# Attention, then a mixture of experts: five key chunks of each first tile of a pair and four of each second one are transposed by DMA, one and two by TensorE

## The chip, the cores and the metric

The kernel runs on one core of a Trainium2 chip. A time is the device time of one execution in microseconds (us); less is better. Of the runs of a kernel the median counts. A profiled execution, which has a time of its own, gave the trace.

## The reference

`q` holds 4 x 12288 queries of width 128. `kv` (4 x 384 x 32 x 128) is averaged over 4 x 4 blocks, which leaves 768 keys a batch, and multiplied by `w_sr`; the result serves as keys and as values. Then a top-1 mixture of experts with 8 experts follows on the 49152 rows.

```python
kv_flat = kv.reshape(B, H // 4, 4, W // 4, 4, C).mean(axis=(2, 4)).reshape(B, -1, C) @ w_sr
s = (q @ kv_flat.transpose(0, 2, 1)) / np.sqrt(C)
a = np.exp(s - s.max(-1, keepdims=True))
a /= a.sum(-1, keepdims=True) + 1e-09
x = (a @ kv_flat).reshape(B * S, D)
do_compute = x @ w_skip > 0
e = argmax(x @ w_gate); gate = softmax(x @ w_gate)[e]
out = x + do_compute * gate * (relu(x @ w1[e]) @ w2[e])
```

## The kernel before

The attention stage goes over 384 tiles of 128 queries, 96 a batch. Everything is kept to nearly float32 precision by splitting operands into a high and a low part, so one product becomes three matmuls. In step t of the loop the program records, in this order on each engine: the scores of tile t (`scores`, TensorE, six matmuls L636 to L638 into `s_ps`, two PSUM buffers); the value product of tile t-6 (`attend`, 18 matmuls, L701); the TensorE transposes of tile t-1 (`p_transpose`, L676); the row maximum of tile t on VectorE (`row_max`, L644, `nm`); the high part of tile t-1 on ScalarE (`p_hi`, L654); the exponential of tile t on ScalarE (`row_exp`, L650, `p_sb`); the low part of tile t-1 on VectorE (`p_lo`, L658), and behind it, on SyncE's queue, a DMA that transposes (L663). The order is the program's own; a schedule is not searched.

The value product needs the 128 x 768 probabilities of a tile transposed, in six chunks of 128 keys. They go two ways. Of the first `KD` = 4 chunks `p_hi` and `p_lo` make a float16 high and low part in a staging tile (`p16`, written `p` in the trace, four buffers), and one DMA transposes both, eight blocks of 128 x 128, into `pt` (six buffers), which `attend` reads six steps later. The other two chunks TensorE transposes in float32 into a PSUM tile that the two tiles of a pair (`PP` = 2) share; one step after the pair is complete ScalarE (L683) and VectorE (L684) split all four of them into high and low float16 parts in `ptq`. So a step with an odd t handles the first tile of a pair in `p_hi` and `p_lo`, and also the `ptq` parts of the pair before.

Between these stand, by rules of the loop, the splits of the queries (L619, L622, each fourth tile), the pooling of the next batch's keys on GpSimd, the routing of finished rows (each twelfth tile) and the scatter of rows to their expert's list (L191, GpSimd). SyncE's queue carries the loads of queries (L605) and keys (L460), the stores of the attention's rows (L719) and the transposing DMAs, in program order.

The second part, from about 960 us on, is the MoE stage: 128-row tiles of each expert's list, `up` (L294 to L298), `down` (L309), `finish` (L321), and its own transposing DMA (`xT<-x`, eight blocks too).

Of the kernel before, what the change touches and what calls it, by code (L numbers as in the profile page):

```python
# [12 lines left out]
F16 = mybir.dt.float16  # L13
# [12 lines left out]
def kernel(  # L26
# [11 lines left out]
    nc = tc.nc  # L38
    NR, C, RT, P = q.shape
    B = kv.shape[0]  # L40
    NQ = NR * RT * P // B
    KC, R = kv.shape[1], kv.shape[2]
# [23 lines left out]
    LAG = 6  # L66
    WARM = 6
    PSL = 11
    KD = 4
    PP = 2  # L70
    L1, L2, PW, PX = 11, 8, 1, 1
    ROW = C + 4
# [14 lines left out]
    ident = consts.tile([P, P], F32, name="ident")  # L87
# [296 lines left out]
    def acc_ps():  # L384
        return ps_a.tile([P, 512], F32, name="acc_ps")
# [34 lines left out]
    with ExitStack() as p1:  # L420
# [7 lines left out]
        ptp = p1.enter_context(tc.tile_pool(name="ptp", bufs=LAG))  # L428
        ptq = p1.enter_context(tc.tile_pool(name="ptq", bufs=4))
        hl = p1.enter_context(tc.tile_pool(name="hl", bufs=4))  # L430
# [167 lines left out]
        q_sb, qT, PT, AVT, ROWS, P_SB, S_PS, P16, PTP, PTQ = ({} for _ in range(10))  # L598
# [51 lines left out]
            nc.scalar.activation(out=P_SB[t], in_=S_PS.pop(t)[:, :, :HK], func=AF.Exp, bias=NM.pop(t))  # L650

        def p_hi(t):
            P16[t] = hl.tile([P, 2, KD * P], F16, name="p16")
            nc.scalar.activation(out=P16[t][:, 0, :], in_=p_flat(t)[:, 0:KD * P], func=AF.Copy, scale=2.0 ** PEXP)  # L654

        def p_lo(t):
            p16 = P16.pop(t)
            paced["both"] = nc.vector.scalar_tensor_tensor(  # L658
                out=p16[:, 1, :], in0=p_flat(t)[:, 0:KD * P], scalar=2.0 ** PEXP, in1=p16[:, 0, :], op0=ALU.mult,
                op1=ALU.subtract).ins  # L660
            P_SB.pop(t)
            PT[t] = ptp.tile([P, 2 * KD, P], F16, name="pt")
            nc.sync.dma_start_transpose(PT[t], p16.rearrange("p a x -> p (a x)"))  # L663

        def p_flat(t):
            return P_SB[t].rearrange("p h x -> p (h x)")

        KP = KC - KD

        def p_transpose(t):  # L670
            g, j = divmod(t, PP)
            if j == 0:
                PTP[g] = acc_ps()
            p = p_flat(t)
            for i in range(KP):
                nc.tensor.transpose(PTP[g][:, (j * KP + i) * P:(j * KP + i + 1) * P],  # L676
                                    p[:, (KD + i) * P:(KD + i + 1) * P], ident)
            if j < PP - 1:
                return
            ps = PTP[g][:, 0:PP * KP * P]  # L680
            hl_t = ptq.tile([P, 2, PP * KP * P], F16, name="ptq")
            PTQ[g] = hl_t.rearrange("p a (j k x) -> p a j k x", j=PP, x=P)
            next_a.append(lambda: nc.scalar.activation(out=hl_t[:, 0, :], in_=ps, func=AF.Copy, scale=2.0 ** PEXP))  # L683
            next_v.append(lambda: nc.vector.scalar_tensor_tensor(  # L684
                out=hl_t[:, 1, :], in0=ps, scalar=2.0 ** PEXP, in1=hl_t[:, 0, :], op0=ALU.mult, op1=ALU.subtract))
# [3 lines left out]
        def attend(t):  # L689
            g, j = divmod(t, GT)  # L690
            r, o = divmod(g, RG)
            v_hi, v_lo, v_sc = *KV[t // TPB][2:4], KV[t // TPB][4][:, 0:1]
            v = (v_hi, v_lo)
            if j % 2 == 0:
                AVT[g] = acc_ps()[:, 0:2 * XW].rearrange("p (a x) -> p a x", x=XW)
            ps = AVT[g]
            pt = PT.pop(t)
            ptq_t = PTQ[t // PP]
            for i, (k, a, x) in enumerate(AVL):
                w = pt[:, x * KD + k, :] if k < KD else ptq_t[:, x, t % PP, k - KD, :]  # L700
                nc.tensor.matmul(ps[:, j % 2, :], w, v[a][:, k, :], start=(i == 0), stop=(i == len(AVL) - 1))  # L701
            if j == 0:
                if o == 0:
                    ROWS[r] = rowp.tile([P, RT, XW], F32, name="rows")
            rows = ROWS[r][:, o * GT:(o + 1) * GT, :]
            rs = small.tile([P, 2], F32, name="rs") if j % 2 == 1 else None

            def inverse():
                nc.vector.tensor_scalar(out=rs, in0=ps[:, :, XW - 1], scalar1=1e-9 * 2.0 ** PEXP, scalar2=v_sc,  # L709
                                        op0=ALU.add, op1=ALU.mult)  # L710
                nc.vector.reciprocal(rs, rs)

            def scale():
                for i in (0, 1):
                    c = j - 1 + i
                    nc.scalar.activation(out=rows[:, c, :], in_=ps[:, i, :], func=AF.Copy, scale=rs[:, i:i + 1])
                if j < GT - 1:
                    return
                nc.sync.dma_start(ov[r][:, o * GT:(o + 1) * GT, :], rows[:, :, 0:C])  # L719
                if o == RG - 1:  # L720
                    jobs.append([route(r), None])

            if j % 2 == 1:
                early_v.append(inverse)
                next_l.append(scale)
# [223 lines left out]
        t = -1  # L949
        while t < NTILE + LAG:  # L950
# [8 lines left out]
            for u in (t - LAG,) if live else (2 * t - NTILE - LAG, 2 * t - NTILE - LAG + 1):  # L959
                if 0 <= u < NTILE:  # L960
                    attend(u)
            if 0 <= t - 1 < NTILE:
                p_transpose(t - 1)
# [4 lines left out]
            if 0 <= t - 1 < NTILE:  # L968
                p_hi(t - 1)
# [5 lines left out]
            if 0 <= t - 1 < NTILE:  # L975
                p_lo(t - 1)
# [135 lines left out]
```

## Time and profile before

| | us |
|---|---|
| runs: median (lowest to highest of 3) | 1744.91 (1743.05 to 1745.06) |
| the profiled execution's own time | 1749.1 |
| its span in the trace | 1747.4 |
| TensorE busy, all of the span | 1703.9 |
| VectorE busy, all of the span | 1533.4 |
| ScalarE busy, all of the span | 1264.5 |
| attention stage, first scores to last | 21 to 958 |

A busy time is the union of an engine's instructions. TensorE's are pipelined with modelled ends, so its busy time says that something was in flight, not that the engine was at its peak.

### The profile page before, as it was taken

The page shows a single profiled execution, that of the slowest core. Times are in us where ns is not written, and L with a number is a line of the kernel's source. Part 1 is how long each engine was busy: PE and PEld are TensorE (multiplying, and loading weights), DVE is VectorE, ACT ScalarE, POOL GpSimd, SP SyncE. Part 2 cuts the span into 40 slices and gives each one's busy share as a digit, 9 for nine tenths or more (in the row PEclk, how much of TensorE's full clock was granted, in tenths as well). Part 3 has the DMA queues.
Part 4 walks back from the last instruction along what each step waited for, and adds up shares of the span by engine and source line. Part 5 has one row for each costly group of instructions (what it writes and reads, how often), then busy time and mean ns, then how long its engine had stood idle before and what let it go on. Part 6 is the DMA issues. An engine that isn't in the chain of part 4 may idle for free.

```text
span 1747.4 us, 51304 instructions
## 1 busy us (share of the span) xinstructions
PE 1703.9 (98%) x18789; PEld 1425.9 (82%) x18789; DVE 1533.4 (88%) x3240; ACT 1264.5 (72%) x2399; POOL 989.9 (57%) x1256
## 2 busy tenths in 40 slices
PE   5999999999999999999999999999999999999998
PEld 3999999999999999999998777777777777777776
DVE  7999999999999999999998777767888888888887
ACT  3888888888888888888888555555566555666664
POOL 2268767888677778565657544444433333334433
PEclk9999999999999999999999999999999999999999
DMA  6999999999799999899998675223433343333333
GB/s 214 236 227 209 201 202 223 226 202 186 171 197 205 224 221 196 186 200 197 204 204 177 161 206 132 85 83 82 94 98 97 100 104 98 97 100 108 99 97 86
DMA packets 616916, 281.18 MB, mean 161 GB/s; under 512 B 502944, under 2 KB 567072, under 8 KB 616736
## 3 DMA queue, kind: packets, MB, share of 16 engines
q1 hardware_dynamic: 590192, 231.68, 64.3%
q0 software_dynamic: 21504, 38.43, 6.8%
q10 hardware_dynamic: 5040, 8.72, 1.3%
q8 instruction: 106, 1.74, 0.4%
q14 instruction: 74, 0.61, 0.1%
HBM read 85.36 MB, written 79.72 MB: 94 GB/s over the span
## 4 chain that ended last, share of the span: by engine, by line
PE 81%; DVE 14%; issue 3%; POOL 1%; DMA 1%; ACT 1%; DVEq 0%; POOLq 0%; SPq 0%; ACTq 0%
PE acc_ps L309 22%; PE acc_ps L701 17%; PE s_ps L636 6%; PE s_ps L638 5%; PE s_ps L637 5%; PE h_ps L294 5%; PE h_ps L295 5%; PE h_ps L296 5%; DVE nm L644 5%; PE acc_ps L676 3%; DVE p L658 3%; PE up_ps L294 2%; PE up_ps L295 2%; PE up_ps L296 2%; DVE ptq L684 2%
## 5 line engine op out<-in xcount | busy, mean ns | idle before, releaser
L191 POOL DMA_INDIRECT scr<-rows,di x384 | 422.8, 1101 | 205.9 <-DVE nm L644 133.0
L650 ACT ACTIVATE p_sb<-s_ps,nm 128x768 f32<-128x768 f32 x384 | 346.4, 902 | 116.5 <-DVE nm L644 103.8
L644 DVE TENSOR_REDUCE nm<-s_ps 128x1 f32<-128x768 f32 x384 | 365.5, 952 | 23.2 <-PE s_ps L638 10.5
L191 POOL DMA_INDIRECT out_dram<-o,xin x196 | 201.4, 1028 | 315.5 <-DVE o L321 266.9
L297 ACT ACTIVATE h_hi<-h_ps 128x512 f16<-128x512 f32 x384 | 223.9, 597 | 208.0 <-PE h_ps L296 194.3
L701 PEld LDWEIGHTS <-pt 128*128 128x128 f16 x4608 | 274.9, 97 | 63.2 <-issue 62.7
L701 PE MATMUL acc_ps<-v_hi,pt 128*128 128x138 f16 x3072 | 320.4, 224 | 1.4 <-DVE rs L709 0.9
L309 PEld LDWEIGHTS <-h_hi 128*128 128x128 f16 x4608 | 288.0, 98 | 17.6 <-issue 1.7
L636 PE MATMUL s_ps<-k_hi,q_hi 128*128 128x384 f32 x768 | 294.4, 383 | 0.4 <-ACT k_hi L511 0.4
L701 PE MATMUL acc_ps<-v_lo,pt 128*128 128x138 f16 x1536 | 293.1, 223 | 0.0
L658 DVE SCALAR_TENSOR_TENSOR p<-p_sb,p 128x512 f16<-128x512 f32 x384 | 271.3, 706 | 2.4 <-ACT p L654 1.1
L298 DVE SCALAR_TENSOR_TENSOR h_lo<-h_ps,h_hi 128x512 f16<-128x512 f32 x384 | 245.7, 687 | 19.8 <-ACT h_hi L297 17.7
L638 PE MATMUL s_ps<-k_hi,q_lo 128*128 128x384 f32 x768 | 260.2, 339 | 0.0
L637 PE MATMUL s_ps<-k_lo,q_hi 128*128 128x384 f32 x768 | 258.7, 337 | 0.0
L654 ACT ACTIVATE p<-p_sb 128x512 f16<-128x512 f32 x384 | 242.1, 631 | 5.3 <-DMA pt<-p 1.8
L309 PE MATMUL acc_ps<-w_hi,h_lo 128*128 128x128 f16 x2304 | 223.1, 219 | 0.6 <-issue 0.5
L309 PE MATMUL acc_ps<-w_lo,h_hi 128*128 128x128 f16 x2304 | 211.8, 219 | 0.8 <-issue 0.7
L309 PE MATMUL acc_ps<-w_hi,h_hi 128*128 128x128 f16 x2304 | 210.9, 219 | 0.0
L297 ACT ACTIVATE h_hi<-up_ps 128x512 f16<-128x512 f32 x192 | 114.4, 597 | 113.5 <-PE up_ps L296 103.6
L701 PE MATMUL acc_ps<-v_hi,ptq 128*128 128x138 f16 x1536 | 178.1, 223 | 0.0
L321 DVE SCALAR_TENSOR_TENSOR o<-acc_ps,g_sc,xin 128x128 f32<-128x128 f32 x288 | 81.0, 344 | 107.1 <-PE acc_ps L309 107.1
L701 PE MATMUL acc_ps<-v_lo,ptq 128*128 128x138 f16 x768 | 155.0, 223 | 0.0
(190 smaller groups left out, 3367.0 us busy)
## 6 DMA issues: line engine op xcount, KB each, us to landing
q_sb<-in_q_dram SPq DMA_DIRECT2D x96, 256.0 KB
out_dram<-rows SPq DMA_DIRECT2D x96, 256.0 KB
xin<-scr SPq DMA_DIRECT2D x75, 264.0 KB, 2.9
kvt<-in_kv_dram SPq DMA_DIRECT2D x74, 256.0 KB
w_raw<-in_moe_w_dram SPq DMA_DIRECT2D x26, 512.0 KB, 4.0
scr<-pad ACTq DMA_DIRECT2D x32, 264.0 KB
pt<-p SPq DMA_TRANSPOSE x384
scr<-rows,di POOLq DMA_INDIRECT x384
```

The costliest lines, as they stand in the source:

```text
L191: ins = nc.gpsimd.indirect_dma_start(out=dst, out_offset=bass.IndirectOffsetOnAxis(ap=ids, axis=0), in_=src, in_offset=None, bounds_check= ...
L297: nc.scalar.activation(out=h["hi"][:, c, :], in_=ps, func=AF.Relu)
L298: paced["by"] = nc.vector.scalar_tensor_tensor(out=h["lo"][:, c, :], in0=ps, scalar=0.0, in1=h["hi"][:, c, :], op0=ALU.max, op1=ALU.subtra ...
L309: m = nc.tensor.matmul(ys[t], h[x][:, k, t * P:(t + 1) * P], w[:, k, :], start=(i == 0), stop=(i == len(terms) - 1))
L636: nc.tensor.matmul(s[:, h, :HK], q_hi, k_hi[:, sl], start=True, stop=False)
L637: nc.tensor.matmul(s[:, h, :HK], q_hi, k_lo[:, sl], start=False, stop=False)
L638: nc.tensor.matmul(s[:, h, :HK], q_lo, k_hi[:, sl], start=False, stop=True)
L644: paced["by"] = nc.vector.tensor_reduce(out=NM[t], in_=S_PS[t][:, :, :HK], axis=AX.XY, op=ALU.max, negate=True).ins
L650: nc.scalar.activation(out=P_SB[t], in_=S_PS.pop(t)[:, :, :HK], func=AF.Exp, bias=NM.pop(t))
L654: nc.scalar.activation(out=P16[t][:, 0, :], in_=p_flat(t)[:, 0:KD * P], func=AF.Copy, scale=2.0 ** PEXP)
L658: paced["both"] = nc.vector.scalar_tensor_tensor(out=p16[:, 1, :], in0=p_flat(t)[:, 0:KD * P], scalar=2.0 ** PEXP, in1=p16[:, 0, :], op0=A ...
L701: nc.tensor.matmul(ps[:, j % 2, :], w, v[a][:, k, :], start=(i == 0), stop=(i == len(AVL) - 1))
```

## The change

The number of chunks that the DMA transposes becomes a list over the place in the pair, `KDS = (5, 4)`, where it was 4 for both. A first tile then has one chunk left for TensorE, a second one two, so a pair's PSUM tile has three chunks where it had four. The tiles `p16` and `pt` are allocated at the larger size, 2 x 5 x 128 columns, and a second tile uses a part of them; `ptq` is allocated for three chunks.

```diff
-    KD = 4
+    KDS = (5, 4)
...
         def p_hi(t):
-            P16[t] = hl.tile([P, 2, KD * P], F16, name="p16")
+            KD = KDS[t % PP]
+            P16[t] = hl.tile([P, 2 * max(KDS) * P], F16, name="p16")[:, 0:2 * KD * P].rearrange("p (a x) -> p a x", a=2)
...
-            PT[t] = ptp.tile([P, 2 * KD, P], F16, name="pt")
+            PT[t] = ptp.tile([P, 2 * max(KDS), P], F16, name="pt")[:, 0:2 * KD, :]
...
-        KP = KC - KD
+        KP0 = [sum(KC - KDS[i] for i in range(j)) for j in range(PP + 1)]
...
-            for i in range(KP):
-                nc.tensor.transpose(PTP[g][:, (j * KP + i) * P:(j * KP + i + 1) * P],
-                                    p[:, (KD + i) * P:(KD + i + 1) * P], ident)
+            for i in range(KP0[j], KP0[j + 1]):
+                k = KDS[j] + i - KP0[j]
+                nc.tensor.transpose(PTP[g][:, i * P:(i + 1) * P], p[:, k * P:(k + 1) * P], ident)
...
-            ps = PTP[g][:, 0:PP * KP * P]
-            hl_t = ptq.tile([P, 2, PP * KP * P], F16, name="ptq")
+            ps = PTP[g][:, 0:KP0[PP] * P]
+            hl_t = ptq.tile([P, 2, KP0[PP] * P], F16, name="ptq")
...
-                w = pt[:, x * KD + k, :] if k < KD else ptq_t[:, x, t % PP, k - KD, :]
+                KD = KDS[t % PP]
+                w = pt[:, x * KD + k, :] if k < KD else ptq_t[:, x, KP0[t % PP] + k - KD, :]
```

The program's instructions before and after have the same places on VectorE and on SyncE's queue. On VectorE, in the middle of the attention stage, three steps before (`p` is the staging tile, `nm` the row maximum, `rs` the scale of finished rows):

```order
1006 L644 TENSOR_REDUCE nm<-s_ps 128x1
1007 L684 SCALAR_TENSOR_TENSOR ptq<-acc_ps,ptq 128x512
1008 L709 TENSOR_SCALAR rs<-acc_ps,v_x_sc 128x2
1009 L711 RECIPROCAL rs<-rs 128x2
1010 L658 SCALAR_TENSOR_TENSOR p_11172<-p_sb,p_11172 128x512
1011 L644 TENSOR_REDUCE nm<-s_ps 128x1
1012 L658 SCALAR_TENSOR_TENSOR p_11222<-p_sb,p_11222 128x512
```

and the same rows now:

```order
1006 L644 TENSOR_REDUCE nm<-s_ps 128x1
1007 L686 SCALAR_TENSOR_TENSOR ptq<-acc_ps,ptq 128x384
1008 L712 TENSOR_SCALAR rs<-acc_ps,v_x_sc 128x2
1009 L714 RECIPROCAL rs<-rs 128x2
1010 L660 SCALAR_TENSOR_TENSOR p_11061<-p_sb,p_11061 128x640
1011 L644 TENSOR_REDUCE nm<-s_ps 128x1
1012 L660 SCALAR_TENSOR_TENSOR p_11111<-p_sb,p_11111 128x512
```

The 128 columns left one instruction of a step and joined another of the same step; the next step is as it was.

On SyncE's queue, a stretch with loads of keys, queries and stores of rows between the transposing DMAs, before:

```order
202 L663 DMA_TRANSPOSE pt<-p_5571 128x8x128
203 L719 DMA out_dram<-rows 128x4x128
204 L663 DMA_TRANSPOSE pt<-p_5620 128x8x128
205 L460 DMA kvt<-in_kv_dram 128x512
206 L663 DMA_TRANSPOSE pt<-p_5670 128x8x128
207 L663 DMA_TRANSPOSE pt<-p_5715 128x8x128
```

and now:

```order
202 L665 DMA_TRANSPOSE pt<-p_5516 128x10x128
203 L722 DMA out_dram<-rows 128x4x128
204 L665 DMA_TRANSPOSE pt<-p_5565 128x8x128
205 L460 DMA kvt<-in_kv_dram 128x512
206 L665 DMA_TRANSPOSE pt<-p_5614 128x10x128
207 L665 DMA_TRANSPOSE pt<-p_5659 128x8x128
```

No DMA changes its place; each other one of the transposes has ten blocks where it had eight.

## Rows read from the trace of the kernel before

**Rows 1.** The page, busy us of each engine, its share of the span, instructions.
```profile
PE 1703.9 (98%) x18789; PEld 1425.9 (82%) x18789; DVE 1533.4 (88%) x3240; ACT 1264.5 (72%) x2399; POOL 989.9 (57%) x1256
```
**Rows 2.** Busy time of each engine in two stretches, granted clock, DMA share, GB/s.
```profile
core 0: us, PE busy (x) PEld busy (x) DVE busy (x) ACT busy (x) POOL busy (x), PEclk, DMA share, GB/s
40.50:917.80 877.30, 873.33 (x9523) 811.50 (x9521) 837.80 (x1640) 761.88 (x1401) 619.39 (x836) 1.00 1.02 205
917.80:958.00 40.20, 36.79 (x397) 33.67 (x394) 35.62 (x75) 32.85 (x64) 29.64 (x39) 1.00 0.90 177
```
**Rows 3.** The same view for the row maximum, L644, alone, with its count.
```profile
40.50:917.80 877.30, 344.18 (x362) 1.00 1.02 205
```
**Rows 4.** Chain that ended last, by line: 40.5:917.8, 285:314, 254.2:464.3, 917:960 us.
```profile
by line: PE acc_ps L701 32.3%; PE s_ps L636 10.7%; PE s_ps L638 10.6%; PE s_ps L637 10.4%; DVE nm L644 8.0%; PE acc_ps L676 6.5%; DVE p L658 5.2%; issue 4.0%; DVE ptq L684 2.9%; DVE q_lo L622 2.0%; DMA pt<-p 0.8%; POOL scr L191 0.7%; POOL e
by line: PE acc_ps L701 46.4%; PE s_ps L636 14.8%; PE s_ps L638 14.5%; PE s_ps L637 14.4%; PE acc_ps L676 9.8%; PE acc_ps L786 0.2%; PE acc_ps L785 0.2%
by line: DVE nm L644 19.4%; PE acc_ps L701 17.5%; DVE p L658 12.3%; issue 7.2%; DVE ptq L684 7.1%; PE s_ps L636 5.6%; PE s_ps L638 5.5%; PE s_ps L637 5.5%; DVE q_lo L622 4.8%; PE acc_ps L676 3.4%; POOL ev L747 2.6%; POOL scr L191 1.9%; DVE 
by line: DVE nm L644 23.3%; issue 13.5%; PE acc_ps L701 9.5%; DVE p L658 9.4%; DVE ptq L684 8.3%; DVE q_lo L622 5.3%; PE s_ps L638 4.7%; PE s_ps L636 4.2%; PE s_ps L637 4.0%; PE acc_ps L676 2.6%; POOL ev L747 2.6%; ACT p_sb L650 2.2%; DVE x
```
**Rows 5.** That chain in order of time, 500:510 us: start us, us, what.
```profile
502.98 1.09 PE acc_ps L701 x18
504.07 0.22 PE acc_ps L676 x2
504.30 0.18 PE s_ps L636
...
505.35 1.09 PE acc_ps L701 x18
```
**Rows 6.** Groups by line and shape: busy us, mean ns of one, idle before, releasers.
```profile
L644 DVE TENSOR_REDUCE nm<-s_ps 128x1 f32<-128x768 f32 x384 | 365.5, 952 | 23.2 <-PE s_ps L638 10.5 <-issue 7.8 <-PE acc_ps L701 3.2
L658 DVE SCALAR_TENSOR_TENSOR p<-p_sb,p 128x512 f16<-128x512 f32 x384 | 271.3, 706 | 2.4 <-ACT p L654 1.1 <-DMA pt<-p 1.0 <-issue 0.3
L654 ACT ACTIVATE p<-p_sb 128x512 f16<-128x512 f32 x384 | 242.1, 631 | 5.3 <-DMA pt<-p 1.8 <-issue 0.4 <-ACT q_hi L619 0.2
L676 PE MATMUL acc_ps<-ident,p_sb 128*128 128x128 f32 x768 | 148.3, 275 | 3.8 <-ACT p_sb L650 3.6
L684 DVE SCALAR_TENSOR_TENSOR ptq<-acc_ps,ptq 128x512 f16<-128x512 f32 x192 | 130.5, 680 | 0.3
L683 ACT ACTIVATE ptq<-acc_ps 128x512 f16<-128x512 f32 x192 | 112.8, 588 | 0.0
L283 DVE SCALAR_TENSOR_TENSOR x<-xin,x 128x128 f16<-128x128 f32 x296 | 84.2, 345 | 0.7 <-ACT x L280 0.7
L321 DVE SCALAR_TENSOR_TENSOR o<-acc_ps,g_sc,xin 128x128 f32<-128x128 f32 x288 | 81.0, 344 | 107.1 <-PE acc_ps L309 107.1
L274 DVE SCALAR_TENSOR_TENSOR w_lo<-w_raw,w_sc,w_hi 128x1024 f16<-128x1024 f32 x13 | 16.7, 1283 | 3.9 <-issue 3.6 <-ACT w_hi L273 0.3
```
**Rows 7.** ScalarE ahead of an exponential: waits 100:900 us in total; timeline of one.
```profile
ACT p_sb L650 <- DVE nm L644: 84.8, 211, 1.5
...
501.64 0.90 ACT L650 ACTIVATE p_sb<-s_ps,nm 128x768 f32<-128x768 f32 x1 [0.43 <-DVE nm L644]
```
**Rows 8.** Transposing DMAs: issue on SyncE ns, a key load, landing, waits 100:900.
```profile
L663 SPq DMA_TRANSPOSE pt<-p x88: 1231/1248/3040, 255.2 to 462.5; - x88
...
291.37 0.57 SPq L460 DMA_DIRECT2D kvt<-in_kv_dram  x1
...
xT<-x SPq DMA_TRANSPOSE x74, 3.4
...
ACT p L654 <- DMA pt<-p: 1.8, 2, 1.3
```

More of the change, by code (lines that the diff above doesn't have):

```diff
@@ L674, in p_transpose @@
             p = p_flat(t)
-            for i in range(KP):
-                nc.tensor.transpose(PTP[g][:, (j * KP + i) * P:(j * KP + i + 1) * P],
-                                    p[:, (KD + i) * P:(KD + i + 1) * P], ident)
+            for i in range(KP0[j], KP0[j + 1]):
+                k = KDS[j] + i - KP0[j]
+                nc.tensor.transpose(PTP[g][:, i * P:(i + 1) * P], p[:, k * P:(k + 1) * P], ident)
             if j < PP - 1:
                 return
-            ps = PTP[g][:, 0:PP * KP * P]
-            hl_t = ptq.tile([P, 2, PP * KP * P], F16, name="ptq")
-            PTQ[g] = hl_t.rearrange("p a (j k x) -> p a j k x", j=PP, x=P)
+            ps = PTP[g][:, 0:KP0[PP] * P]
+            hl_t = ptq.tile([P, 2, KP0[PP] * P], F16, name="ptq")
+            PTQ[g] = hl_t.rearrange("p a (k x) -> p a k x", x=P)
             next_a.append(lambda: nc.scalar.activation(out=hl_t[:, 0, :], in_=ps, func=AF.Copy, scale=2.0 ** PEXP))
@@ L699, in attend @@
             for i, (k, a, x) in enumerate(AVL):
-                w = pt[:, x * KD + k, :] if k < KD else ptq_t[:, x, t % PP, k - KD, :]
+                KD = KDS[t % PP]
+                w = pt[:, x * KD + k, :] if k < KD else ptq_t[:, x, KP0[t % PP] + k - KD, :]
                 nc.tensor.matmul(ps[:, j % 2, :], w, v[a][:, k, :], start=(i == 0), stop=(i == len(AVL) - 1))
```

## The prediction

> **What bounds the kernel now.** I read the page first: TensorE is busy for 98% of the span, VectorE for 88%, so two engines are candidates [rows 1]. The change touches only the attention stage, and the table of stretches cuts that out: from 40.5 to 917.8 us of the span TensorE is busy for 873.3 of 877.3 us, VectorE for 837.8, ScalarE for 761.9 [rows 2]. VectorE's row maximum runs once for every tile of 128 queries and 362 times in that stretch [rows 3], so a tile takes 877.3 / 362 = 2.42 us on average, of which VectorE works 837.8 / 362 = 2.31 us. A busy TensorE is no proof that it sets the pace, since its ends are modelled and overlap. The chain that ended last decides that: the reader should add up its shares by engine. In the stretch, TensorE's five lines hold 32.3 + 10.7 + 10.6 + 10.4 + 6.5 = 70.5%, VectorE's four largest 8.0 + 5.2 + 2.9 + 2.0 = 18.1%, the rest is issue, DMA and GpSimd [rows 4]. It is not even: from 285 to 314 us the chain never leaves TensorE, from 254 to 464 us VectorE holds the larger part, and at the stage's end, from 917 to 960 us, TensorE has only 9.5 + 4.7 + 4.2 + 4.0 + 2.6 = 25.0% [rows 4]. The pieces of the chain in order of time show one tile on TensorE: 18 value matmuls 1.09 us, two transposes 0.22 us, six score matmuls of some 0.175 us, and 505.35 - 502.98 = 2.37 us from one tile to the next [rows 5]. So VectorE is a close second, never far behind: it has 0.11 us a tile to spare on average.
>
> **The change, part by part.** *TensorE* loses one of four transposes a pair. The two of a tile take 0.22 us of the chain, thus 0.11 us each [rows 5]. Bounds: the value matmuls go 18 in 1.09 us, 0.061 us each at 138 columns, so a 128-column pass is hardly under 0.056 us; and if the one that goes were the dear one of the two, with 0.056 left for the other, it would be 0.22 - 0.056 = 0.164 us. No row shows a transpose that stands alone. I take 0.11: the two are alike, and the middle of the bounds is there too. There are 384 tiles, 192 pairs: 192 x 0.11 = 21.1 us of TensorE's work goes.
>
> The group of transposes has a mean of 275 ns [rows 6], which is how long one is in flight, not how far apart two stand. The Trainium skill, page "TensorE: Matmul & The Clock Gate", section "Part 4: PE-mode transpose", gives about 275 ns for one in a kernel's context; the trace agrees with that as a duration (275 ns), but the chain charges 0.11 us. By the page's figure the change would free 192 x 0.275 = 52.8 us, by the chain 21.1 us, and I go by the chain.
>
> *What of it reaches the end.* A saving on TensorE moves the end only where TensorE carries the chain. 181 of the pairs lie in the stretch: 181 x 0.11 x 0.705 = 14.0 us. In the last 15 tiles it is 7.5 x 0.11 x 0.25 = 0.2 us, in the first 7 tiles, which wait for the first keys, I count nothing. The gain is 14.2 us.
>
> *VectorE* does the low half of the split of the first tile over 640 columns where it did 512, and the low half of the pair's TensorE chunks over 384 where it did 512. The 512-column one takes 706 ns, the same operation over 1024 columns 1283 and over 128 columns 345 [rows 6]: (1283 - 706) / 512 = 1.13 and (706 - 345) / 384 = 0.94 ns a column, so +120 to +144 ns. The other reads PSUM: 680 ns at 512 columns, 344 for a like one at 128 [rows 6], 0.875 ns a column, so -112 ns. No row has the 384-column one itself. VectorE's net is +8 to +33 ns a pair, I take 20. Both stand in the same step, the one that handles a first tile, so no step of VectorE gets heavier by more than that. In the 18.1% of the chain that VectorE holds this costs 192 x 0.020 x 0.181 = 0.7 us; elsewhere its spare 0.11 us a tile covers it.
>
> *ScalarE* has the high halves of the same two splits, 631 and 588 ns now [rows 6]. From no gain on the second and a fully proportional price on the first, 631 x 128 / 512 = 158 ns, to a net of nothing: 0 to +158 ns a pair, in the same step. Ahead of each exponential it idles for the row maximum, 84.8 us in 211 waits between 100 and 900 us, 0.43 us in the tile shown [rows 7]. That hides it; without that cover half of the bound would cost 192 x 0.08 = 15 us.
>
> *DMA and its queue.* The transposing DMA of a first tile grows by a quarter, from 2 x 4 to 2 x 5 blocks. Issuing it holds SyncE's queue for 1.25 us in the median now, so about 1.55 us after (estimate, in proportion) [rows 8]. For twelve tiles the queue issues 12 transposes and some ten plain loads and stores at 0.57 us: 15.0 + 5.7 = 20.7 us now, 22.6 us after, in 12 x 2.42 = 29.1 us now and about 28.2 us then [rows 3, 8]. It fits. Landing: no row shows this DMA's own time to land, but the MoE stage's transpose of the same 128 x 1024 size lands after 3.4 us in the median [rows 8]. Its staging buffer is needed again four tiles, 9.5 us, after it was first written, and its result six tiles after. Even 3.4 x 1.25 = 4.3 us behind a whole step of 2.4 us leave over 2 us. Between 100 and 900 us ScalarE waited twice, 1.8 us in all, for such a buffer [rows 8]; I charge nothing. The DMA engines' share reads 1.02 and 205 GB/s over the stretch [rows 2]; 181 x 65.5 KB more in 877 us are 13.5 GB/s.
>
> *Nothing else moves:* the 18 value matmuls of a tile stay, three of them a pair read the DMA's result in place of TensorE's; the MoE stage has the same instructions.
>
> **Sum:** -14.2 + 0.7 = -13.5 us. Against the profiled execution's 1749.1 us that is 1735.6 us; the runs' median is 1744.9 us, so a median of 1731.4 us, -0.8%.
>
> **The rivals.** *VectorE takes over.* The row maximum, the one instruction of VectorE that waits for TensorE, has 23.2 us of idle time ahead of it in 384 tiles, 0.06 us a tile [rows 6]; the rest of the spare 0.11 us may be short gaps between dependent instructions that no faster TensorE removes. TensorE's saving of 0.055 us a tile and VectorE's own 0.01 us then use up all there is, and the stretches that are TensorE's now turn into VectorE's. For: from 254 to 464 us it carries the chain already. Against: from 285 to 314 us the chain has no VectorE piece. If a third of the gain is left: 14.2 / 3 = 5 us, 1740 us.
>
> *The transposing DMA comes late (slower).* In a stretch where SyncE's queue is also loading keys, a first tile's DMA is issued a step late, takes over 4.6 us to land, and the high half four tiles on waits on its staging buffer; scores queue behind, since the exponential stands behind that on ScalarE. For: it happened, up to 1.3 us at a time, and the DMA piece in the chain is 0.8% of 877 us, 7 us [rows 4, 8]. Its queue's longest issue is 3.04 us. Against: two times in 800 us. It decides once there are 14 such waits of 1 us; with 20 the time is 1744.9 - 13.5 + 20 = 1751 us. The Trainium skill, page "DMA: Bandwidth & Descriptors", section "Latency and other measured facts", gives an effective rate of 261 GB/s for a DMA transpose; no row here isolates that rate. By that figure one would take 1.26 us for the larger transpose (an estimate from the page), still inside a tile.
>
> *It does nothing that can be told:* TensorE's transposes are in truth hidden behind the loads of weights that the next scores need anyway, and the score matmuls start where they started. For: a transpose is in flight for 0.275 us and the chain charges 0.11, so more than half of it is covered already [rows 5, 6]. Against: on the stretches that are TensorE's the chain steps through both transposes in each tile. Time: 1745 us, give or take 3.5.
>
> **How the numbers follow.** What a measurement of this kernel can tell from no change is about 0.2%, 3.5 us. My forecast, a gain of 8 to 20 us, gets 0.66; VectorE's takeover, 3.5 to 8 us, 0.13; more than 20 us, up to all of TensorE's 21 us and something for shorter waits, 0.04; no difference 0.07; slower 0.10. So faster 0.83, same 0.07, slower 0.10. The range 1723 to 1741 us leaves out the last two cases and half of the largest gain, 0.19 in all. The low price of a transpose (0.056 us) gives a gain of 14.2 x 0.056 / 0.11 - 0.7 = 6.5 us, 1738 us, the high one (0.164 us) 14.2 x 0.164 / 0.11 - 0.7 = 20.5 us, 1724 us, and both lie in it.
>
> **What the changed profile would show.** Right: from one tile to the next TensorE's chain alternates between about 2.26 and 2.37 us; the first tile's low half near 0.84 us and the pair's near 0.57 us; VectorE's busy share of the attention stage up from 95.5% to about 97%, and its share of the chain up; ScalarE's waits for the transposing DMA still a handful; the MoE stage as long as before. Wrong, if the step with one transpose is hardly shorter than that with two (hidden), if VectorE's lines hold most of the chain from 40 us on (takeover), or if waits on the staging buffer recur in each round of twelve tiles (late DMA).

## The result and the profile after

The changed kernel takes 1757.3 us (median of 4 runs, 1755.6 to 1762.6) beside 1744.0 us before (4 runs, 1741.8 to 1745.1): a ratio of 1.0083, 95% interval 1.0058 to 1.0108. It is slower, by about 13 us, where 13.5 us of gain were forecast. The profiled execution took 1762.6 us, the slowest of the four; its span is 1760.9. It lies 13.5 us above the profiled execution before (1749.1), so the two traces show the same loss as the medians.

The page's busy times and the chain by engine, after:

```profile
PE 1697.7 (96%) x18597; PEld 1409.8 (80%) x18597; DVE 1543.7 (88%) x3240; ACT 1264.9 (72%) x2399; POOL 1028.1 (58%) x1256
PE 72%; DVE 17%; issue 4%; DMA 3%; ACT 2%; POOL 2%; DVEq 0%; POOLq 0%; SPq 0%; ACTq 0%
```

Beside [rows 1] TensorE has 192 transposes less and only 6 us less of busy time, VectorE 10 us more with as many instructions, GpSimd 38 us more with as many instructions, and GpSimd's code was not touched. Of these 38 us the scatters hold 14.0 (422.8 us before), the key adds 9.9 (104.6 before), and most of the rest is small operations of the routing. From the first score matmul of the first tile to that of the last the attention stage took 937.0 us and now takes 953.7; what lies behind it fell from 789.4 to 786.2.

The loss has places. The table gives the time of twelve tiles, from the first score matmul of tile k to that of tile k + 12, worked out from the traces, before, after, and for the experiments told below (some rounds of 32):

```
k      before  after  pace_alone  width_alone  dma_eight  no_pooling_adds  low_narrow  mn_step_later
12      28.63  29.96       27.91        29.07      27.91            29.14       27.91          31.15
24      28.63  30.31       27.91        29.16      27.91            29.18       27.91          29.51
36      28.94  31.98       28.97        31.69      27.96            33.28       27.93          29.17
60      28.81  30.38       27.91        30.41      30.39            27.91       29.51          29.34
96      28.61  27.95       27.95        28.59      27.95            27.95       27.95          27.92
108     28.55  27.95       27.95        29.01      27.95            27.95       27.95          27.95
132     28.55  30.08       27.97        30.09      30.09            28.05       27.97          27.96
156     28.76  30.17       29.31        30.10      30.16            27.97       29.25          28.67
216     28.63  30.11       27.93        30.12      30.14            27.93       27.93          29.09
228     28.67  30.08       27.91        30.09      30.10            28.18       27.91          28.42
264     28.68  30.39       29.58        30.40      29.35            27.91       29.59          29.18
312     28.55  27.97       27.97        28.57      27.97            27.97       27.97          28.00
360     30.48  31.29       30.51        31.40      31.50            31.50       30.65          31.25
stage  937.0  953.7      920.9        957.3      940.5            927.5       926.5          936.7
```

There are three kinds of rounds. In the thirteen that got faster the sum is -7.3 us; most of them take 27.95 us where they took 28.6, 0.6 to 0.65 us less, six transposes of 0.11. In the thirteen from 48 to 264 that got slower, all of them rounds in which GpSimd pools keys, the sum is +16.3 us; call such a round *jammed*. The three rounds 12, 24 and 36, in which the second batch's keys are loaded, cost +6.1 us. Two near the stage's end, 348 and 360, cost +1.7. Together +16.8, the stage's 16.7 to rounding (round 180 changed by 0.04).

The stretches, after: the stage without its ends; the three early rounds; a round that got faster (108); a jammed one (132):

```profile
core 0: us, PE busy (x) PEld busy (x) DVE busy (x) ACT busy (x) POOL busy (x), PEclk, DMA share, GB/s
41.30:934.60 893.30, 866.45 (x9338) 794.34 (x9336) 846.51 (x1639) 761.61 (x1400) 657.40 (x836) 1.00 1.08 215
53.70:146.00 92.30, 86.47 (x929) 78.46 (x926) 79.15 (x155) 74.67 (x138) 46.73 (x70) 1.00 1.15 228
294.80:322.80 28.00, 28.00 (x313) 26.07 (x310) 27.18 (x55) 25.50 (x48) 22.69 (x32) 1.00 1.18 265
351.90:382.00 30.10, 28.93 (x312) 26.23 (x310) 28.55 (x54) 25.28 (x48) 26.95 (x32) 1.00 1.06 204
```

and the chain by line in the last three of them, in the order 294.8 to 322.8, 351.9 to 382.0, 53.7 to 146 us:

```profile
by line: PE acc_ps L704 47.1%; PE s_ps L636 15.4%; PE s_ps L638 15.1%; PE s_ps L637 14.9%; PE acc_ps L679 7.5%; PE acc_ps L788 0.2%; PE acc_ps L789 0.2%
by line: PE acc_ps L704 33.2%; DVE nm L644 12.1%; PE s_ps L636 9.4%; PE s_ps L638 9.4%; PE s_ps L637 9.3%; PE acc_ps L679 6.3%; DVE q_lo L622 5.0%; issue 3.9%; DVE ptq L686 3.1%; POOL ev L750 2.9%; POOL d L750 2.7%; DVE p L660 2.3%; DVE rs 
by line: DMA pt<-p 39.8%; PE acc_ps L704 15.7%; PE s_ps L636 6.1%; PE s_ps L637 5.5%; PE s_ps L638 5.5%; ACT p_sb L650 4.5%; PE acc_ps L679 4.1%; DVE nm L644 3.8%; issue 3.5%; DVE p L660 2.4%; ACT p L655 2.3%; ACT rows L719 1.9%; DVE q_lo L
```

In the quiet round TensorE carries the chain alone and VectorE works 27.18 of 28.00 us: the forecast's 97% (from 41.3 to 934.6 us it is 94.8%, less than the 95.5% before). In the jammed round VectorE's busy time rises by 1.37 us with one instruction less, GpSimd's by 4.26 with as many; TensorE is idle for 1.17 us of it. The six adds account for 0.92 of the 4.26 us (5.32 after 4.40), the scatters for 1.45 with one less. In the early rounds neither engine sets the pace: 40% of the chain is the transposing DMA, and VectorE works 79.15 of 92.30 us. The granted clock reads 1.00 in all of these.

### The profile page after: what moved, and what is told of

Same layout as the page of the kernel before. It is cut to its first block, busy times and chain, and to the rows that moved or that the text cites. A ratio compares the mean times of both kernels' runs of the same rounds, so it can differ in the third digit from the quotient of the medians.

```text
span 1760.9 us, 50920 instructions
## 1 busy us (share of the span) xinstructions
PE 1697.7 (96%) x18597; PEld 1409.8 (80%) x18597; DVE 1543.7 (88%) x3240; ACT 1264.9 (72%) x2399; POOL 1028.1 (58%) x1256
## 4 chain that ended last, share of the span: by engine, by line
PE 72%; DVE 17%; issue 4%; DMA 3%; ACT 2%; POOL 2%; DVEq 0%; POOLq 0%; SPq 0%; ACTq 0%
PE acc_ps L309 22%; PE acc_ps L704 13%; DVE nm L644 7%; PE h_ps L294 5%; PE h_ps L295 5%; PE h_ps L296 5%; PE s_ps L636 4%; PE s_ps L638 4%; PE s_ps L637 4%; DVE p L660 3%; PE acc_ps L679 2%; DMA pt<-p 2%; PE up_ps L294 2%; PE up_ps L296 2%; PE up_ps L295 2%
## 5 line engine op out<-in xcount | busy, mean ns | idle before, releaser
L191 POOL DMA_INDIRECT scr<-rows,di x384 | 436.8, 1137 | 185.8 <-DVE nm L644 103.5
L644 DVE TENSOR_REDUCE nm<-s_ps 128x1 f32<-128x768 f32 x384 | 364.6, 949 | 10.1 <-PE s_ps L638 8.6
L704 PEld LDWEIGHTS <-pt 128*128 128x128 f16 x5184 | 310.1, 98 | 70.7 <-issue 65.7
L704 PE MATMUL acc_ps<-v_hi,pt 128*128 128x138 f16 x3456 | 355.1, 224 | 6.9 <-DVE rs L712 4.0
L704 PE MATMUL acc_ps<-v_lo,pt 128*128 128x138 f16 x1728 | 327.9, 223 | 0.0
L660 DVE SCALAR_TENSOR_TENSOR p<-p_sb,p 128x640 f16<-128x640 f32 (+1 forms) x384 | 308.3, 803 | 12.7 <-ACT p L655 12.0
L655 ACT ACTIVATE p<-p_sb 128x640 f16<-128x640 f32 (+1 forms) x384 | 262.8, 684 | 23.5 <-DMA pt<-p 20.4
L485 POOL TENSOR_TENSOR kvt<-kvt 128x256 f32<-128x256 f32 x133 | 114.5, 862 | 65.9 <-DVE p L660 51.2
L309 PEld LDWEIGHTS <-h_lo 128*128 128x128 f16 x2304 | 152.8, 98 | 0.0
```

The source lines that it names most:

```text
L191: ins = nc.gpsimd.indirect_dma_start(out=dst, out_offset=bass.IndirectOffsetOnAxis(ap=ids, axis=0), in_=src, in_offset=None, bounds_check= ...
L309: m = nc.tensor.matmul(ys[t], h[x][:, k, t * P:(t + 1) * P], w[:, k, :], start=(i == 0), stop=(i == len(terms) - 1))
L644: paced["by"] = nc.vector.tensor_reduce(out=NM[t], in_=S_PS[t][:, :, :HK], axis=AX.XY, op=ALU.max, negate=True).ins
L660: paced["both"] = nc.vector.scalar_tensor_tensor(out=p16[:, 1, :], in0=p_flat(t)[:, 0:KD * P], scalar=2.0 ** PEXP, in1=p16[:, 0, :], op0=A ...
```

## Where the jammed rounds lose it

The groups by shape that answer to [rows 6], of the whole kernel after:

```profile
L660 DVE SCALAR_TENSOR_TENSOR p<-p_sb,p 128x640 f16<-128x640 f32 x192 | 169.2, 881 | 5.9 <-ACT p L655 5.6 <-ACT p_sb L650 0.3
L660 DVE SCALAR_TENSOR_TENSOR p<-p_sb,p 128x512 f16<-128x512 f32 x192 | 139.2, 725 | 6.8 <-ACT p L655 6.4
L686 DVE SCALAR_TENSOR_TENSOR ptq<-acc_ps,ptq 128x384 f16<-128x384 f32 x192 | 104.9, 546 | 0.0
L685 ACT ACTIVATE ptq<-acc_ps 128x384 f16<-128x384 f32 x192 | 92.5, 482 | 0.0
L644 DVE TENSOR_REDUCE nm<-s_ps 128x1 f32<-128x768 f32 x384 | 364.6, 949 | 10.1 <-PE s_ps L638 8.6
L191 POOL DMA_INDIRECT scr<-rows,di x384 | 436.8, 1137 | 185.8 <-DVE nm L644 103.5 <-issue 31.9 <-DVE ids L326 9.1
L485 POOL TENSOR_TENSOR kvt<-kvt 128x256 f32<-128x256 f32 x133 | 114.5, 862 | 65.9 <-DVE p L660 51.2 <-DMA kvt<-in_kv_dram 7.2 <-DVE q_lo L622 4.3
```

The reader is to see that the row maximum, which reads PSUM, has not changed (949 ns, before 952), while the low half of a second tile, still 512 columns (725 ns, before 706), GpSimd's key adds (862, before 788) and its scatters (1137, before 1101) have all become longer. The 640-column low half has a mean of 881 ns; in the quiet round 108 it is 830, near the forecast.

The two engines in order of time, after, from a quiet stretch (296.7 to 298 us) and from jammed ones:

```profile
296.74 0.72 POOL L485 TENSOR_TENSOR kvt<-kvt 128x256 f32<-128x256 f32 x1
297.43 0.68 DVE L660 SCALAR_TENSOR_TENSOR p<-p_sb,p 128x512 f16<-128x512 f32 x1
...
343.04 0.82 DVE L660 SCALAR_TENSOR_TENSOR p<-p_sb,p 128x640 f16<-128x640 f32 x1
343.10 1.62 POOL L191 DMA_INDIRECT scr<-rows,di  x1 [0.17 <-DVE rs L712]
344.74 0.80 POOL L750 TENSOR_TENSOR d<-rows,mx 128x96 f32<-128x96 f32 x1
346.18 0.39 POOL L750 TENSOR_TENSOR ev<-ev,em 128x96 f32<-128x96 f32 x1
346.60 0.25 DVE L764 TENSOR_REDUCE mn<-ev 128x12 f32<-128x96 f32 x1 [1.27 <-POOL ev L750]
...
355.20 0.73 DVE L660 SCALAR_TENSOR_TENSOR p<-p_sb,p 128x512 f16<-128x512 f32 x1
355.31 1.19 POOL L485 TENSOR_TENSOR kvt<-kvt 128x256 f32<-128x256 f32 x1
```

At 296.74 the add has 0.03 us left when the low half begins, and both take their usual time. At 355.31 the add begins 0.11 us into a low half and takes 1.19 us in place of 0.72: it ends 0.57 us behind the low half's end. At 343.10 a scatter begins under a low half and takes 1.62 us; the routing behind it on GpSimd is late, and `mn` on VectorE waits 1.27 us for `ev`, with the next row maximum behind it in VectorE's queue and the next exponential behind that.

That this is a rule shows in all of the adds between tile 48 and tile 360, sorted by whether a VectorE instruction with two operands in SBUF (`p_lo` or `q_lo`) was running when the add began; counted from the traces, mean ns (count):

```
                                 before      after       low_narrow  dma_eight   pace_alone
add begun while one ran          1189 (15)   1186 (37)   1170 (22)   1190 (34)   1190 (14)
all other adds                    740 (89)    740 (67)    742 (82)    741 (70)    740 (90)
```

An add that begins second takes 430 to 450 ns more in these five kernels. The end says it more sharply: before, all 15 such adds end 580 to 590 ns behind the end of the VectorE instruction that they began under; after, 36 of the 37 end 573 to 596 ns behind it, with 542 to 757 ns of it still to run when they began (the other began under a `q_lo` and took its usual time). What the change moved is how many begin second: 15 of 104 before, 37 after. It goes the other way too: after, a 640-column low half that begins while an add runs has a mean of 1034 ns (35 of them), one that begins with no GpSimd work running 839 (18). The adds that lose are seldom under the wide half itself: 34 of the 37 began under a second tile's 512-column low half, two under one of 640 columns. VectorE's instructions on PSUM do not care: the row maximum takes 948 ns with GpSimd running and 951 without, the pair's low half 545 and 548. Scatters that begin under such a low half take 1312 ns (147), others 1015 (166); before it was 1242 (135) and 1010 (177).

The kernel has a guard against this: it orders each pooling add and each operation of the routing behind the VectorE low half recorded before it (`behind`, L490). In the quiet round GpSimd waits for it, 0.4 us before `d`. Before the 37 adds GpSimd had stood idle for 0.03 us at most, so none was released by the guard: GpSimd was late, its own low half was over, and it met a later one.

The Trainium skill, page "SBUF — State Buffer", section "SBUF: two separate sides", says that VectorE and GpSimd share one pair of ports, that a VectorE instruction with two SBUF inputs takes it against a GpSimd instruction that reads SBUF, and that whichever starts first has it for the whole instruction while the other fully blocks. For the adds the trace agrees (740 against 1186 ns, ends 573 to 596 ns behind VectorE's, and PSUM readers untouched). For the scatters it does not fit as well: a low half of 640 columns that begins while a scatter runs takes 834 ns in the mean, no longer than alone, and only 15 of the 153 low halves that begin so take 0.98 to 1.35 us.

Waits in the stage that grew, 100 to 900 us, after:

```profile
ACT p_sb L650 <- DVE nm L644: 95.5, 231, 1.3
PEld acc_ps L679 <- ACT p_sb L650: 20.0, 38, 1.0
DVE mn L764 <- POOL ev L750: 17.4, 23, 1.3
ACT p L655 <- DMA pt<-p: 13.2, 13, 2.5
```

`mn` waited as often before, 6.5 us in all. The last row answers to [rows 8]: two waits of 1.8 us in all before, thirteen now, and twenty over the whole stage, 20.4 us.

## The experiments

Two theories at first. *Width:* VectorE's wider low half, an instruction with two SBUF operands, makes VectorE and GpSimd run into each other more often, and this costs the jammed rounds. *DMA:* the ten-block transpose is late, as the slower rival of the forecast had it. A third, *pace*, was that a faster TensorE alone uncovers this or another bound.

**pace_alone** keeps TensorE's three transposes a pair and leaves the fifth chunk out of the high half, the low half and the DMA; the product reads the fourth chunk twice. The first edit stands in both `p_hi` and `p_lo`.

```diff
-            KD = KDS[t % PP]
+            KD = min(KDS)
...
-                w = pt[:, x * KD + k, :] if k < KD else ...
+                w = pt[:, x * min(KDS) + min(k, min(KDS) - 1), :] if k < KD else ...
```

> Leaves out: the fifth chunk of a first tile is neither split nor transposed by DMA, and the value product uses the fourth chunk twice in its place. So TensorE does three transposes a pair as in the changed kernel, while the staging tile, its two halves and the DMA are as before (512 columns, eight blocks) and the pair's own split has 384 columns. Pace theory (a shorter step of TensorE alone jams VectorE and GpSimd in the rounds of twelve tiles with key pooling): rounds 48, 60, 120 to 168, 216 to 264 still take about 30 us and the time is 1745 us or more. Width theory (the 640-column halves collide with GpSimd's pooling): no jam, all rounds near 27.9 us, 1724 to 1731 us. DMA theory (the ten-block DMA comes late): the same 1724 to 1731 us, since the DMA is as before.

Measured: 1730.0 us beside 1743.4, ratio 0.9930 (0.9912 to 0.9949). **width_alone** does the reverse: it keeps the wide split and the ten blocks, and puts a fourth TensorE transpose back, into PSUM columns that nothing reads.

```diff
+                nc.tensor.transpose(PTP[g][:, KP0[PP] * P:(KP0[PP] + 1) * P], p[:, (KC - 2) * P:(KC - 1) * P], ident)
```

> The changed kernel with a fourth transpose a pair put back on TensorE, into columns that nobody reads, so that each tile has two as before; the 640-column halves, the 384-column split and the ten-block DMA stay. Pace theory: the jam goes, 1742 to 1748 us. Width theory: the jam stays in the rounds with key pooling, about 30 us each, and the quiet rounds are back at 28.6 us: 1760 to 1768 us. DMA theory: late in rounds 12 to 36 as in the changed kernel but not elsewhere, 1748 to 1755 us.

Measured: 1766.2 us beside 1743.4, ratio 1.0126 (1.0108 to 1.0145). So the transpose saved is worth 13.4 us with no chunk added, and the added work costs 23 us with nothing saved: the change is a gain as large as forecast and a larger loss. (pace_alone spares VectorE some 0.13 us a pair too, since the pair's split has 384 columns and the low half still 512, so the 13.4 us are the worth of both.) The rounds of the table agree: 27.9 us nearly everywhere in the one, 30.1 us in the same rounds as after in the other. In width_alone 36 of 104 adds begin under a low half, in pace_alone 14: the wide half brings the overlaps, the faster TensorE alone does not. Yet pace is not wholly innocent: four rounds of pace_alone (156, 168, 252, 264) are jammed as well, at 28.8 to 29.6 us.

**dma_eight** does all of the change but the larger DMA, which transposes eight of a first tile's ten blocks; the product reads the eighth for the last two.

```diff
-            nc.sync.dma_start_transpose(PT[t], p16.rearrange("p a x -> p (a x)"))
+            nc.sync.dma_start_transpose(PT[t][:, 0:2 * min(KDS), :], p16.rearrange("p a x -> p (a x)")[:, 0:2 * min(KDS) * P])
```

> Leaves out: of a first tile's ten blocks the DMA transposes the first eight, and the value product reads the eighth in place of the last two. All else as in the changed kernel, the 640-column halves and three transposes a pair included. DMA theory for everything: 1724 to 1732 us. DMA theory for rounds 12 to 36 only (they cost 6 us there): these rounds fall from 30.0, 30.3 and 32.0 us to about 28, the jammed rounds stay at 30 us, 1748 to 1752 us. Width or pace theory for all of it: 1755 to 1759 us.

Measured: 1753.4 us beside 1743.4, ratio 1.0057 (1.0038 to 1.0076), between two of the expectations; the trace is of the fastest execution, 1747.6 us. The early rounds are the fast 27.9 us, the jammed ones as jammed as after but for two, 48 (29.4 us) and 264 (29.4):

```profile
52.10:135.90 83.80, 83.80 (x928) 78.10 (x926) 79.26 (x155) 75.18 (x138) 48.77 (x71) 1.00 1.15 240
341.30:371.40 30.10, 28.98 (x310) 26.23 (x309) 28.55 (x54) 25.27 (x47) 26.99 (x32) 1.00 1.02 193
```

So the DMA is the cause in rounds 12 to 36, and by the same sign in round 348 (28.3 us here; after, 29.4, with a piece of 6.80 us of this DMA in the chain at 905.93), and most of the loss is not its. **low_narrow** goes one step further than dma_eight: the first tile's low half on VectorE covers 512 columns, and the fifth chunk's low half is left out; ScalarE's high half stays at 640.

```diff
-                out=p16[:, 1, :], in0=p_flat(t)[:, 0:KD * P], scalar=2.0 ** PEXP, in1=p16[:, 0, :], op0=ALU.mult,
+                out=p16[:, 1, 0:min(KDS) * P], in0=p_flat(t)[:, 0:min(KDS) * P], scalar=2.0 ** PEXP,
+                in1=p16[:, 0, 0:min(KDS) * P], op0=ALU.mult,
```

> Leaves out, on top of the run with the eight-block DMA, the low half of the fifth chunk: VectorE's low half of a first tile has 512 columns again, ScalarE's high half still 640, three transposes a pair. If VectorE's 640-column low half starts the jam: rounds 120 to 264 near 27.95 us but for the few that jam in the run with TensorE's pace alone, 1726 to 1733 us. If the width on ScalarE or the larger tiles' places in memory matter: as the run with the eight-block DMA, 1748 to 1755 us.

Measured: 1734.2 us beside 1747.7, ratio 0.9915 (0.9899 to 0.9932). 128 columns of one VectorE instruction, 0.14 us a pair by the quiet rows or some 27 us of VectorE's time in all, decide between +10.0 us (dma_eight) and -13.5, each against the kernel before, measured beside it. Six rounds stay jammed without the wide low half: 156, 168, 252 and 264, as in pace_alone, and 48 and 60 (28.9 to 29.6 us). The same round as above is quiet, with GpSimd at 22.45 us where it had 26.99:

```profile
340.00:367.90 27.90, 27.90 (x311) 25.96 (x309) 26.96 (x54) 24.90 (x47) 22.45 (x31) 1.00 1.03 213
L485 POOL TENSOR_TENSOR kvt<-kvt 128x256 f32<-128x256 f32 x6 | 4.5, 744 | 0.1
```

**no_pooling_adds** (one run) takes the other partner away: from the changed kernel GpSimd's pooling adds of batches 1 to 3 are left out, all but the last. The keys are then wrong and the expert lists may differ, so only the attention rounds count.

```diff
-            n = R * R * C
+            n = R * R * C if b == 0 else 2 * C
```

> Leaves out, for batches 1 to 3, GpSimd's adds that pool the keys, but the last one: the keys are wrong, and the expert lists and with them the MoE stage may change length, so only the attention stage's rounds of twelve tiles count. All else is the changed kernel. If the jam is GpSimd's queue running full (theory: the 640-column halves lengthen GpSimd's adds, GpSimd becomes the bound): rounds 48 to 60, 120 to 168 and 204 to 264 fall to about 27.95 us, rounds 12 to 36 stay at 30 to 32 us (the late DMA). If VectorE alone is the bound, with its 640-column halves, they stay near 30 us.

Measured: 1738.7 us beside 1747.7. With the wide low half and the faster TensorE in place the rounds that were jammed go at 27.9 to 28.9 us, and the 640-column low half is back at 826 ns (the second row is round 132):

```profile
L660 DVE SCALAR_TENSOR_TENSOR p<-p_sb,p 128x640 f16<-128x640 f32 x189 | 156.1, 826 | 1.9 <-issue 1.4 <-ACT p L655 0.3
346.20:374.30 28.10, 28.10 (x312) 26.09 (x310) 27.27 (x55) 25.37 (x47) 17.45 (x25) 1.00 1.17 227
```

The early rounds stay late (29.1, 29.2, 33.3 us), as they should if they are the DMA's. Width's partner is thus GpSimd: the wide low half alone, with VectorE at 27.27 of 28.10 us, does not jam a round. The wide half is not needed for every jam, as the rounds of pace_alone and low_narrow show; with it there are thirteen, without it four and six. No run gives VectorE the same 0.14 us a pair in an instruction that reads PSUM, so how much of the 23.5 us is the collision and how much the plain length is not separated. Nor is it shown for GpSimd whether the overlap or its load counts for more, since both go with the adds.

**mn_step_later** asks what part is the wait of `mn`: it records `mn` one step later in a round.

```diff
+            if r < SNAPR - 1:
+                yield
```

> Nothing is left out. The changed kernel with the route's reduction that waits for GpSimd (mn) taken one step later, so that VectorE does not stand still for it (1.27 us in each jammed round). If that wait is what costs: jammed rounds fall by 1 to 1.3 us to 28.8 to 29, 1742 to 1746 us. If GpSimd's full queue sets the jam's pace: the wait goes, the rounds stay within 0.4 us of 30 us, 1753 to 1758 us.

Measured: 1753.6 us beside 1747.7, ratio 1.0036 (1.0021 to 1.0050). The wait is gone (0.8 us in 3 times, from 17.4 in 23), and most jammed rounds fall to 27.9 to 29.6 us, few all the way, while 120 and 144 do not fall: 30 of 103 adds still begin under a low half. Both parts of a jam are real, the wait and the longer instructions. The stage is 936.7 us, but the part behind it is 792.1 us in place of 786.2, which is not explained.

The rest asked whether the gain can be kept. **five_where_quiet** uses five and four only for tiles 72 to 119, 180 to 203 and 276 to 347, else four and four, and leaves nothing out:

```diff
+    FIVE = (range(72, 120), range(180, 204), range(276, 348))
+        def kds(t):
+            return KDS if any(t // PP * PP in r for r in FIVE) else (min(KDS),) * PP
```

> Nothing is left out. Five and four chunks only for the tiles of rounds that the changed kernel runs faster (72 to 119, 180 to 203, 276 to 347), four and four elsewhere. All theories: the nine to eleven quiet rounds keep their gain of 0.6 us each and the others are as before, 1736 to 1740 us. If a jam once begun is carried by something else than the rounds' own work, 1744 us or more.

Measured: 1740.4 us (10 runs) beside 1743.4, ratio 0.9985 (0.9976 to 0.9995). Some rounds with four and four got longer all the same, the most 120 (29.3 us for 28.6, with 4.6 us of the transposing DMA in its chain), 240 (30.6 for 29.8) and 252 (30.2 for 28.6); for the last two the cause is not shown. **pooling_spread** has five and four from tile 72 on and one key load each 10/3 tiles in place of 3:

```diff
+    FIVE = (range(72, NTILE),)
-                at = 7 * i // 4 if nb == 1 else (nb - 1) * TPB - 10 + 3 * i
+                at = 7 * i // 4 if nb == 1 else (nb - 1) * TPB - 10 + 10 * i // 3
```

> Nothing is left out. Five and four chunks from tile 72 on, four and four before it, and the key loads of batches 2 and 3 at every 3.33 tiles in place of every third, so GpSimd's adds are spread over 80 steps in place of 72. If GpSimd's load per round decides: 7 to 10 of the eleven jammed rounds fall to 28 us, 1732 to 1738 us. If a tenth less is not enough: rounds 120 to 168 and 204 to 264 stay near 30 us, 1745 to 1752 us.

Measured: 1754.9 us beside 1747.7, ratio 1.0040 (1.0027 to 1.0053). A miss: the adds spread by a tenth still jam (29.1 to 30.4 us in nine of the eleven rounds, 240 is longer and 264 quiet). **five_fewer** has five and four in fewer rounds still,

```diff
+    FIVE = (range(72, 108), range(180, 192), range(276, 336))
```

> Nothing is left out. Five and four chunks only for tiles 72 to 107, 180 to 191 and 276 to 335, so the last round before each dense stretch of key pooling is back at four and four. If the jam is started by 640-column halves beside the pooling: no round above its time before, ten rounds with 0.4 to 0.8 us less, 5 to 6 us faster than before. If the jam, or the loss at 120, 240 and 252, comes without them: 2 to 3 us faster, as in the first try.

and took 1744.3 us beside 1748.1, ratio 0.9979 (0.9969 to 0.9988): a gain of 0.2%, as small as five_where_quiet's and short of the 5 to 6 us expected. Those two beat both kernels, hardly. **five_fewer_mn** adds the later `mn` to it.

> Nothing is left out. The run before this one, with the route's reduction that waits for GpSimd one step later for all but the last rounds. If VectorE's 0.28 us of standing for it in every round of before is on the way: 31 rounds x up to 0.2 us more, 8 to 11 us faster than before. If VectorE's wait is covered where TensorE sets the pace: the same 5 to 6 us.

A miss: 1752.5 us beside 1748.1, ratio 1.0030 (1.0018 to 1.0042). Its stage takes 935.9 us where five_fewer's takes 931.2, the rest 793.3 in place of 787.7: the later `mn` goes with about 5.6 us behind the stage, as in mn_step_later, and 4.7 us in it. **four_then_five** (one run) gives the fifth chunk to the second tile of a pair.

```diff
-    KDS = (5, 4)
+    KDS = (4, 5)
```

> Nothing is left out. Four chunks for the first tile of a pair and five for the second: the 640-column halves move to the step in which VectorE splits the queries too, the 384-column split stays in the other. If only the width beside GpSimd's adds matters: jammed rounds as in the changed kernel, 1752 to 1760 us. If the balance within a step matters: VectorE's fuller step stretches also the quiet rounds, over 28.1 us in place of 27.95, and the time is 1760 us or more.

Measured: 1768.6 us beside 1748.1. Round 72, quiet with (5, 4), is jammed too (30.3 us). Round 96 takes 29.9 us, but with no add begun under a low half and 7.9 us of the transposing DMA in its chain. Of the rounds without pooling 288 to 312 stay near 27.95, 324 and 336 take 28.3 and 28.8. Its 36 adds that begin under a low half, here the 640-column one, take 1327 ns. In its step the second tile has no narrower low half of a pair to pay for the wider one.

## Why the prediction was wrong

*TensorE, 0.11 us a pair: right.* The chain of the quiet stretch, in order of time, steps from product to product by 300.76 - 298.49 = 2.27 and 303.12 - 300.76 = 2.36 us, as forecast:

```profile
298.49 1.10 PE acc_ps L704 x18
299.58 0.11 PE acc_ps L679
...
300.76 1.09 PE acc_ps L704 x18
301.85 0.22 PE acc_ps L679 x2
...
303.12 1.09 PE acc_ps L704 x18
```

The term of 14.2 us that reach the end is near too, pace_alone measured 13.4, but in part by luck: the forecast let TensorE's share of the chain, 70.5%, stand for what is saved, while in pace_alone nearly every round got shorter, also most of those from 254 to 464 us, by 16.4 us in all, and the four jammed ones gave 2.4 us back. VectorE's relief there is in it as well.

*VectorE: the step that failed.* "No step of VectorE gets heavier by more than that ... elsewhere its spare 0.11 us a tile covers it", priced at 0.7 us. The lengths of the instructions were right in quiet rounds (0.83 and 0.55 us against the forecast's 0.84 and 0.57), the net was small, and yet low_narrow beside dma_eight shows that 128 columns of it are worth 10.0 + 13.5 = 23.5 us. The sum added two prices as if they were of one kind. The 128 columns went from an instruction that reads PSUM, whose length GpSimd does not change (545 and 548 ns), to one with two SBUF operands, which holds GpSimd's adds up or is held up by them; so while VectorE's work stayed level, the part of it that collides rose by a tenth, 1.37 to 1.51 us a pair. At the same time the tile became 0.055 us shorter, so VectorE's spare time fell to (28.00 - 27.18) / 12 = 0.07 us a tile. GpSimd, 57% busy over the span [rows 1], was nowhere in the argument as a party; but in the pooling rounds it is busy for 80% (22.9 us of 28.6, round 108 before), 90% in a jammed one (26.95 of 30.10). The forecast's chain of 254 to 464 us, with VectorE ahead and GpSimd's `ev` and scatter in it [rows 4], held the sign: rounds 48, 144 and 156 of before already had adds of 0.97 us in the mean, three of six begun under a low half, only without the loss. That TensorE was slow enough to hide it is an inference; `mn` waited 0.28 us in those rounds, not 1.27.

*DMA: the second step that failed.* "It fits ... I charge nothing." The mean over twelve tiles was compared, 22.6 us of queue in 28.2, with a landing of 4.3 us. In the early rounds neither holds. SyncE's queue there, after, a piece of the chain, and the waits from 53.7 to 146 us (the last row is SyncE's own):

```profile
111.45 1.23 SPq L665 DMA_TRANSPOSE pt<-p  x1
112.73 0.57 SPq L605 DMA_DIRECT2D q_sb<-in_q_dram  x1
113.41 1.31 SPq L665 DMA_TRANSPOSE pt<-p  x1
114.77 0.58 SPq L460 DMA_DIRECT2D kvt<-in_kv_dram  x1
115.44 0.41 SPq L722 DMA_DIRECT2D out_dram<-rows  x1
115.95 5.91 SPq L665 DMA_TRANSPOSE pt<-p  x2
...
115.95 6.86 DMA pt<-p
...
ACT p L655 <- DMA pt<-p: 14.0, 12, 2.8
DVE p L660 <- ACT p L655: 10.0, 10, 2.5
...
SPq L665 <- PE acc_ps L704: 22.1, 15, 3.9
```

The queue has no break between its loads, and two transposes in it take 5.91 us; part of that is not SyncE's work but its wait for TensorE's value product (the last row, from the end of the instruction before; 13.6 us in 13 times from 54.1 to 140.3 us before), so a late transpose and a late product go together, and which came first is not shown. The chain's six pieces of this DMA there, from issue to landing, are 4.7 to 7.0 us long, where 4.3 us were forecast; before, with eight blocks, the chain has one such piece in these rounds and it is as long (6.99 us, at 121.36), so the 3.4 us borrowed from the MoE stage did not hold here even for the smaller size. With that, the staging buffer is not free when `p_hi` needs it, and ScalarE waits 14.0 us in twelve places. The rival named this mechanism, its place (rounds that load keys) and its threshold, 14 waits of 1 us; 20 came, of 20.4 us, but some are hidden, and rounds 12 to 36 cost 6 us. It was not the larger loss: dma_eight takes it away and is still at 1.0057.

*The other rivals.* "VectorE takes over" is nearest to what happened, but it left a third of the gain, 1740 us: it had VectorE's rows at their old lengths. In the jammed round VectorE's 28.55 us and `mn`'s wait of 1.27 fill 29.82 of 30.10 us: it has next to no time to spare, with rows that are longer than in the quiet round, though TensorE's five lines still carry 67.6% of that round's chain. "Does nothing" is refuted by pace_alone. ScalarE is covered as forecast: its high half of 640 columns takes 737 ns in the mean, and its waits for the row maximum grew.

*The MoE stage* was to stay as long; what lies behind the attention stage took 786.2 us for 789.4.

**Open:** round 360's +0.8 us, in which no keys are pooled (31.3 us; 30.5 and 30.7 in pace_alone and low_narrow, but 31.2 in five_where_quiet, which has four and four there); why the later `mn` goes with 5 to 6 us behind the stage; why rounds 240 and 252 lengthen in five_where_quiet; and how an early collision keeps a round in the jam. That the wider instruction brings more overlaps is counted; what one add under one low half costs was counted in place, not run by itself.

## What to carry to other kernels

Price a moved piece of VectorE work by where its operands lie, not by its length alone: in this kernel columns that moved from a PSUM reader to an instruction with two SBUF operands began to collide with GpSimd, and both engines' work became longer. When a change shortens the step, ask of each engine that is 80% busy or more in some stretch what it will do at the new pace, GpSimd and the queue of SyncE too, and in the fullest stretch, not in the mean. A share of the chain tells where a gain can be had, not that nothing else is a few hundredths of a us behind it.

## What was not expected of the hardware

GpSimd's add of 128 x 256 float32 has two durations, 740 and 1186 ns, and which it takes hangs on whether a `p_lo` or `q_lo` of VectorE began before it; a held add ends about 0.58 us behind that instruction's end, however much of it was left. Of the changed kernel's twelve-tile rounds with key pooling most take about 27.95 or about 30.1 us, but overlaps alone do not make a slow one: round 144 of pace_alone has three of six adds begun under a low half and takes 28.04 us. What the rounds near 30.1 have besides is `mn`'s wait of 1.27 us for GpSimd, in place of 0.28.
